# Block-diagonal attention with stationary probabilities, and batches 0 and 1 in 512-byte rows with f32 weights cast on chip

## The chip, the cores and the metric

The kernel runs on one core of one Trainium2 chip. The metric is the time of one execution in device microseconds. Before the change it took 377.15 us (median of three runs, 373.92 to 379.12).

Short names: PE is TensorE, DVE is VectorE, ACT is ScalarE, POOL is GpSimd, SP is SyncE, which here only issues DMAs. A *pass* is one matmul of 512 columns.

## The reference

Sliding-window attention over 8 batches of 8 heads, 576 positions and head size 64 (a position sees 32 positions to each side), then a dense layer pair with a squared relu.

```python
scores = q @ k.T / 8;  scores = where(|i - j| <= 32, scores, -1e9)
x = softmax(scores) @ v                   # (8, 8, 576, 64) -> 4608 tokens x 512
h = maximum(x @ w_in, 0)                  # 512 -> 2048
out = (s * h * h + b) @ w_out             # 2048 -> 512, s and b are one number each
```

q, k and v are drawn as 0.1 times a normal, so the scores are near zero and the softmax near uniform.

The constant `b` gives every token the same row `b * sum(w_out)`, called the constant row below (`CVEC`).

## The kernel before

The kernel does not write its instructions in order. It describes tasks (engine, cost, what they read and write), and a list scheduler in the kernel's own Python turns them into one fixed order per engine. The costs in the tasks decide the order; nothing is reordered when the kernel runs. Every engine works through its order and waits on semaphores.

```python
def plan(self):                           # before; [...] marks cuts
    [...]
    c = (max(free[s], t.ready), t.key, t.n)          # earliest start first
    [...]
    free[t.stream] = st + t.cost
    if t.dma is not None:                            # one DMA queue is modelled
        dma_free = max(dma_free, st + 1300.0) + t.dma[1]
        t.fin = dma_free + 700.0
    [...]

def load(b, n, blk, stream="sp", waits=()):          # q, k, v: 128 rows of 8 x 256 B
    [...]
    1070.0 if stream != "pool" else 1900.0, [...]
def load_weights(which, i, waits=()):                # POOL, f32 -> bf16 in the load
    e.dma_start(WIN_BF[:, :, i*512:(i+1)*512], moe_w_in[...])
def transpose_dma(b, n, blk):                        # q, k of batches 1 to 7, on SP
    e.dma_start(dst[:, :, s0:s0+ns], NAT[n][0:ns, blk, :], transpose=True)   # cost 1300

def unit(b, t, g2, after):                # 48 of them: 192 queries, 4 heads
    # PE: 8 matmuls q x k (64 rows deep)      -> SC
    # ACT: exp(SC) -> EX;  DVE: EX *= MASK
    # PE: 8 matmuls ONES x EX -> SS (the sums, 64 columns of weights)
    # PE: 8 matmuls V x EX    -> AV (already transposed: channels x tokens)
    # ACT: ln(SS), exp(-ln) -> REC;  DVE: XT = AV * REC
    [...]

def s1(m, ft): # PE: 4 passes w_in x XT -> W; ACT: relu -> R1; DVE: R1*R1 -> GT
def s2(m, sub, qd): # PE: 4 passes GT x w_out -> O; after 16: DVE -> OUTS, SP stores
```

The dense layers run over token blocks: 384, 128, then 512 tokens each. "The third block" is the first of 512 tokens.

The softmax here doesn't subtract the row's maximum and nothing guards it: scores larger than these inputs give would overflow.

Of the kernel before, what the change touches and what calls it, by code (L numbers as in the profile page):

```python
# [5 lines left out]
F32 = mybir.dt.float32  # L6
# [4 lines left out]
S = 576  # L11
# [6 lines left out]
NBLK = (S + 127) // 128  # L18
KCOLS = NBLK * 128
TOK = 512  # L20
# [4 lines left out]
class _Task:  # L25


    __slots__ = ("n", "stream", "fns", "cost", "lat", "key", "deps", "after", "users", "left",
                 "ready", "start", "fin", "dma", "sem", "seq", "val", "used", "snap")

    def __init__(self, n, stream, fns, cost, lat, key, dma):
        self.n, self.stream, self.fns, self.cost, self.lat, self.key, self.dma = \
            n, stream, fns, cost, lat, key, dma
        self.deps, self.after, self.users = set(), [], []
        self.ready = self.start = self.fin = 0.0
        self.sem = self.seq = self.val = None
        self.used = False
        self.snap = None


class _Graph:
# [3 lines left out]

    STREAMS = ("pe", "act", "dve", "pool", "sp")
    LAT = {"pe": 230.0, "act": 110.0, "dve": 90.0, "pool": 120.0, "sp": 60.0}

    def __init__(self, queues):
        self.queues = queues  # L50
        self.tasks = []
        self.writer, self.readers, self.named = {}, {}, {}

    def add(self, stream, fns, cost, reads=(), writes=(), key=0.0, accum=False, dma=None, waits=(),
            after=(), name=None, lat=None):


        if not isinstance(fns, list):
            fns = [fns]
        t = _Task(len(self.tasks), stream, fns, cost, self.LAT[stream] if lat is None else lat, key,  # L60
                  dma)
# [10 lines left out]
        t.after = list(after)  # L72
# [6 lines left out]
        if name is not None:  # L79
            self.named[name] = t  # L80
# [3 lines left out]
    def plan(self):  # L84
        free = {s: 0.0 for s in self.STREAMS}
        dma_free = 0.0
        for t in self.tasks:
            aft = [self.named[a] for a in t.after]
            t.left = len(t.deps) + len(aft)
            for d in t.deps:  # L90
                d.users.append((t, True))
            for d in aft:
                d.users.append((t, False))
        open_ = {s: [] for s in self.STREAMS}
        for t in self.tasks:
            if t.left == 0:
                open_[t.stream].append(t)
        order = []
        while len(order) < len(self.tasks):
# [10 lines left out]
            free[t.stream] = st + t.cost  # L110
            if t.dma is not None:
                dma_free = max(dma_free, st + 1300.0) + t.dma[1]
                t.fin = dma_free + 700.0
            else:
                t.fin = st + t.cost
            order.append(t)
            for u, hard in t.users:
                u.left -= 1
                if hard and u.stream == t.stream and t.dma is None and t.stream == "pe":
                    r = t.fin  # L120
                elif hard:
                    r = t.fin + (100.0 if t.dma is not None else t.lat)
                else:
                    r = t.start
                u.ready = max(u.ready, r)
                if u.left == 0:
                    open_[u.stream].append(u)
        self.order = order

    def emit(self, sems):  # L130


# [5 lines left out]
        plan = []  # L138

# [12 lines left out]
        for t in self.order:  # L152
            s = t.stream
            need = {}
            for d in t.deps:
                if s == "pe" and d.stream == "pe" and d.dma is None:
                    continue
                want(s, d, need)
            if t.dma is not None:
# [50 lines left out]
def bass_sliding_window_symmetric__then__act_starrelu_kernel(  # L210
# [12 lines left out]
    NT3 = S // 192  # L223

    sizes = [384, 128]
# [8 lines left out]
    with ExitStack() as es:  # L234
# [6 lines left out]
        def ps(shape, nm, dt=F32):  # L241
            uid["n"] += 1
            return es.enter_context(nc.psum_tensor(f"{nm}_{uid['n']}", list(shape), dt))

        WIN_BF = sb((128, 4, DFF), BF16, "win")
        WOUT_BF = sb((128, 16, DM), BF16, "wout")
        XT = sb((128, NPAIR, T), BF16, "xt")
        STG = {n: sb((128, NBLK, DM), F32, "stg" + n) for n in "qk"}
        STG["v"] = sb((128, 2 * NT3, DM), F32, "stgv")
        NAT = {n: sb((128, NBLK, DM), BF16, "nat" + n) for n in "qk"}  # L250
        VB = [sb((128, 2 * NT3, DM), BF16, "vb") for _ in range(2)]
        QT = [sb((128, NPAIR, S), BF16, "qt") for _ in range(2)]
        KT = [sb((128, NPAIR, S + 2 * WIN), BF16, "kt") for _ in range(2)]
        EX = [sb((128, 2, 512), BF16, "ex") for _ in range(2)]
        MASK = sb((128, 2, 512), BF16, "mask")
        LNS = [sb((128, 384), F32, "lns") for _ in range(2)]
        REC = [sb((128, 384), F32, "rec") for _ in range(2)]
        ONES = sb((128, 3, 64), BF16, "ones")
        ONESW = sb((128, 128), BF16, "onesw")
        IDENT = sb((128, 128), BF16, "ident")  # L260
        ZERO_F = sb((128, 1), F32, "zero")
        GT = [sb((128, 16, 512), BF16, "gt") for _ in range(2)]
        R1 = [sb((128, 512), BF16, "r1") for _ in range(4)]
        OUTS = [sb((128, DM), F32, "outs") for _ in range(3)]
# [6 lines left out]
        AV = ps((128, 512), "av")  # L271
        SS = ps((128, 512), "ss")
        BANKS = {("W", 0): W[0], ("W", 1): W[1], ("O", 0): O[0], ("O", 1): O[1]}

        queues = {"w": [f"dmaW{i}" for i in range(10)], "l": [f"dmaL{i}" for i in range(24)],
                  "a": [f"dmaA{i}" for i in range(8)], "o": [f"dmaO{i}" for i in range(8)],
# [6 lines left out]
        def rows(blk):  # L283
            return min(128, S - blk * 128)


        src_of = {"q": q, "k": k, "v": v}

        def load(b, n, blk, stream="sp", waits=()):
            if n == "v":  # L290
                k0 = 192 * (blk // 2) - WIN + 128 * (blk % 2)
                p0, p1 = max(0, -k0), min(128, S - k0)
                s0 = k0 + p0
            else:
                p0, p1 = 0, rows(blk)
                s0 = 128 * blk
            ns = p1 - p0
            return add(
                stream,
                lambda e: e.dma_start(  # L300
                    STG[n][p0:p1, blk, :].rearrange("p (h d) -> p h d", h=H),
                    src_of[n][b, :, s0:s0 + ns, :].rearrange("h s d -> s h d"),
                ),
                1070.0 if stream != "pool" else 1900.0, writes=[("STG", n, blk)],
                key=16 * (b - 2), waits=waits,
                dma=({"sp": "l", "act": "a", "pool": "w"}[stream], ns * 9.3))

        def load_weights(which, i, waits=()):
            if which == "in":
                fn = lambda e: e.dma_start(  # L310
                    WIN_BF[:, :, i * 512:(i + 1) * 512],
                    moe_w_in.rearrange("(kc p) f -> p kc f", p=128)[:, :, i * 512:(i + 1) * 512])
            else:
                fn = lambda e: e.dma_start(
                    WOUT_BF[:, 4 * i:4 * i + 4, :],
                    moe_w_out.rearrange("(fc p) c -> p fc c", p=128)[:, 4 * i:4 * i + 4, :])
            return add("pool", fn, 1000.0, writes=[("W" + which, i)], waits=waits, key=-50,
                       dma=("w", 2550.0))


        first = {}
        plan0 = [("q", 0, "sp"), ("k", 0, "act"), ("q", 1, "sp"), ("k", 1, "act"), ("v", 0, "sp"),
                 ("v", 1, "act"), ("q", 2, "sp"), ("k", 2, "act"), ("k", 3, "sp"), ("v", 2, "act"),
                 ("v", 3, "sp"), ("q", 3, "act"), ("q", 4, "sp"), ("k", 4, "act"), ("v", 4, "sp"),
                 ("v", 5, "sp")]
        for n, blk, stream in plan0:
            first[n, blk] = load(0, n, blk, stream)

        add("dve", lambda e: e.memset(ZERO_F[:], 0.0), 100, writes=["ZERO"], key=-99)
        add("dve", lambda e: e.memset(ONESW[:], 1.0), 150, writes=["ONESW"], key=-99)  # L330
        add("dve", lambda e: e.memset(ONES[:], 1.0), 150, writes=["ONES"], key=-99)
        add("dve", lambda e: e.memset(ONES[0:WIN, 1, :], 0.0), 100, writes=["ONES"], key=-98)
        add("dve", lambda e: e.memset(ONES[128 - WIN:128, 2, :], 0.0), 100, writes=["ONES"], key=-98)
        for slot in range(2):
            for c0 in (0, WIN + S):
                add("dve", lambda e, slot=slot, c0=c0: e.memset(KT[slot][:, :, c0:c0 + WIN], 0.0), 150,
                    writes=[("KTPAD", slot)], key=-98)
        for (p0, blk) in ((0, 0), (128 - WIN, 2 * NT3 - 1)):
            add("dve", lambda e, p0=p0, blk=blk: e.memset(STG["v"][p0:p0 + WIN, blk, :], 0.0), 350,
                writes=[("STGPAD", blk)], key=-98)  # L340
        add("pool", [lambda e: e.dma_start(SB128[:, 0:1], moe_s.partition_broadcast(128)),
                     lambda e: e.dma_start(SB128[:, 1:2], moe_b.partition_broadcast(128))],
            2000.0, writes=["SB128"], dma=("w", 200.0), key=-60)

        def band(tile, res, lo, hi):

            add("pool",
                lambda e: e.affine_select(tile, ONESW[:, :], pattern=[[1, 128]],
# [68 lines left out]
        def blocks(lo, hi):  # L417
            return range(lo // 128, (hi - 1) // 128 + 1)
# [224 lines left out]
```

## Time and profile before

| | before |
|---|---|
| median of three runs | 377.15 us |
| span of the profiled execution | 373.8 us |
| PE busy | 319.2 us (85%) |
| first 128x512 matmul of the third token block | 99.25 us |
| PE idle before 100 us / from 100 to 260 us | 40.1 / 10.0 us |

From the page of the kernel before: busy time by engine, then two rows of the 40 equal slices of the span (one digit a slice, tenths; `PEclk` is the clock granted to TensorE).

```profile
span 373.8 us, 6108 instructions
...
PE 319.2 (85%) x2385; PEld 155.5 (42%) x2424; DVE 193.2 (52%) x439; ACT 206.4 (55%) x310; POOL 44.7 (12%) x62
...
PE   1277985935499999988898899989999999999996
...
PEclk9999998975599999999999999999999999999999
```

PE is full from about the twelfth slice on. What the kernel loses lies in the first 100 us. The view by windows gives the same in microseconds: the window, its length, busy time (and count) of PE, weight loads, DVE, ACT and POOL, then the granted clock, the DMA share and GB/s.

```profile
0.00:30.00 30.00, 11.33 (x132) 7.75 (x134) 14.30 (x41) 11.30 (x16) 5.31 (x15) 1.00 1.00 164
30.00:60.00 30.00, 24.49 (x170) 12.76 (x168) 10.46 (x27) 16.03 (x29) 8.78 (x11) 1.00 1.16 199
60.00:100.00 40.00, 24.04 (x236) 14.67 (x240) 23.70 (x61) 17.08 (x29) 12.81 (x15) 0.69 1.20 212
100.00:260.00 160.00, 149.99 (x1205) 70.28 (x1224) 101.15 (x228) 110.25 (x161) 17.82 (x21) 0.99 1.03 180
```

PE idle is the window's length less PE busy: 18.7, 5.5, 16.0, then 10.0 us in the 160 us that follow. PE's waits in the kernel before (what waited and for what: total us, times, longest):

```profile
PE ss L458 <- DVE ex L445: 20.1, 13, 2.0
PE w L402 <- DVE natq L379: 6.0, 2, 5.3
...
PE o L543 <- DVE cvec L567: 4.0, 1, 4.0
PE sc L435 <- DMA kt<-natk: 3.7, 2, 2.0
```

11.8 of the 20.1 us are batch 1's six units, one after another between 75 and 97 us. The third block then starts (from the timeline of PE):

```profile
99.25 4.92 PE L525 MATMUL w<-xt,win 128*128 128x512 bf16 x14 [3.27 <-DVE xt L472]
```

### The profile page before, as it was taken

Reading aid. Unit: us, or ns where it says so; the run is one execution under the profiler, and the core shown is the slowest. Engines: PE = TensorE matmul, PEld = TensorE weight load, DVE = VectorE, ACT = ScalarE, POOL = GpSimd, SP = SyncE. Lnnn points to the kernel's source line nnn. Section 1 sums busy time; section 2 is a strip of 40 time slices with the busy share of each in tenths; the row PEclk is TensorE's granted clock in tenths of the full one; section 3 lists DMA queues with packets and bytes.
Section 4 is the critical chain, followed back from the end, with each engine's and each line's share of the span. In section 5 each row is a group of like instructions: output and inputs, shape, how many; then the busy total and the mean of one; then the engine's idle time right before and its main releaser. Section 6 shows DMA issues by size and latency. Waiting matters only on the chain.

```text
span 373.8 us, 6108 instructions
## 1 busy us (share of the span) xinstructions
PE 319.2 (85%) x2385; PEld 155.5 (42%) x2424; DVE 193.2 (52%) x439; ACT 206.4 (55%) x310; POOL 44.7 (12%) x62
## 2 busy tenths in 40 slices
PE   1277985935499999988898899989999999999996
PEld 0144543523244444443444344434444444444442
DVE  4363525745556775676585586454444453333321
ACT  1266732255368678767677576657676764434300
POOL 3012241342221210121111000000000000000000
PEclk9999998975599999999999999999999999999999
DMA  8979999999999999999899798863000001001012
GB/s 164 208 110 187 190 225 206 202 190 213 230 221 147 180 200 231 186 198 193 188 172 213 132 174 174 189 141 89 28 31 31 28 30 56 28 30 56 28 58 84
DMA packets 127869, 52.71 MB, mean 141 GB/s; under 512 B 116672, under 2 KB 120768, under 8 KB 127840
## 3 DMA queue, kind: packets, MB, share of 16 engines
q1 hardware_dynamic: 113648, 36.32, 54.2%
q0 software_dynamic: 7424, 14.29, 19.8%
q10 hardware_dynamic: 6768, 1.70, 2.7%
q8 instruction: 19, 0.31, 0.4%
q14 instruction: 10, 0.08, 0.1%
HBM read 38.80 MB, written 9.44 MB: 129 GB/s over the span
## 4 chain that ended last, share of the span: by engine, by line
PE 54%; DMA 19%; SPq 9%; DVE 7%; ACTq 3%; ACT 3%; issue 2%; DVEq 0%
PE o L543 25%; PE w L525 22%; DMA stgq<-in_q_dram 12%; DMA stgk<-in_k_dram 7%; SPq L300 6%; ACTq L300 3%; SPq L387 3%; PE ss L458 3%; PE sc L435 2%; DVE ex L445 2%; PE av L458 2%; ACT ex L442 1%; DVE xt L472 1%; DVE vb L379 1%; DVE gt L534 1%
## 5 line engine op out<-in xcount | busy, mean ns | idle before, releaser
L525 PE MATMUL w<-xt,win 128*128 128x512 bf16 (+2 forms) x624 | 146.4, 367 | 5.5 <-DVE xt L472 4.2
L543 PE MATMUL o<-wout,gt 128*128 128x512 bf16 x554 | 141.5, 382 | 6.0 <-DVE cvec L567 4.0
L525 PEld LDWEIGHTS w<-xt,win 128*128 128x128 bf16 x640 | 59.4, 100 | 71.8 <-issue 5.1
L543 PEld LDWEIGHTS o<-wout,gt 128*128 128x128 bf16 x576 | 53.2, 98 | 65.5 <-DVE cvec L567 4.2
L442 ACT ACTIVATE ex<-sc,zero 128x1024 bf16<-128x1024 f32 x48 | 53.2, 1109 | 12.1 <-PE sc L435 12.1
L445 DVE TENSOR_TENSOR ex<-ex,mask 128x1024 bf16<-128x1024 bf16 x48 | 33.0, 688 | 33.2 <-ACT ex L442 32.7
L300 POOL DMA_DIRECT2D stgv<-in_v_dram x42 | 35.7, 853 | 120.5 <-DVE vb L379 111.5
L465 ACT ACTIVATE lns<-ss,zero 128x384 f32<-128x384 f32 x48 | 27.7, 578 | 27.6 <-PE ss L458 27.5
L531 ACT ACTIVATE r_29<-w,zero 128x512 bf16<-128x512 f32 (+2 forms) x40 | 25.7, 643 | 30.7 <-PE w L525 30.6
L458 PE MATMUL ss<-ex,ones 128*64 128x128 bf16 x384 | 22.1, 244 | 20.5 <-DVE ex L445 20.1
L531 ACT ACTIVATE r_28<-w,zero 128x512 bf16<-128x512 f32 (+2 forms) x40 | 25.7, 642 | 23.1 <-PE w L525 22.6
L531 ACT ACTIVATE r_31<-w,zero 128x512 bf16<-128x512 f32 (+2 forms) x40 | 25.7, 644 | 23.0 <-PE w L525 22.0
L531 ACT ACTIVATE r_30<-w,zero 128x512 bf16<-128x512 f32 (+2 forms) x40 | 25.7, 643 | 19.2 <-PE w L525 18.8
L555 DVE SCALAR_TENSOR_TENSOR outs<-o,sb_36,cvec 128x512 f32<-128x512 f32 x36 | 26.8, 746 | 13.2 <-PE o L543 12.8
L472 DVE TENSOR_TENSOR xt<-av,rec 128x384 bf16<-128x384 f32 x48 | 26.5, 552 | 11.5 <-ACT rec L468 11.2
L379 DVE CAST natq<-stgq 128x512 bf16<-128x512 f32 (+1 forms) x40 | 17.2, 432 | 25.3 <-DMA stgq<-in_q_dram 25.0
L458 PEld LDWEIGHTS ss<-ex,ones 128*64 128x64 bf16 x384 | 13.6, 119 | 39.6 <-DVE ex L445 26.7
L468 ACT ACTIVATE rec<-lns,zero 128x384 f32<-128x384 f32 x48 | 29.3, 610 | 0.8
L435 PE MATMUL sc<-qt,kt 64*128 64x128 bf16 x384 | 21.2, 237 | 9.0 <-ACT qt L407 5.3
L534 DVE TENSOR_TENSOR gt<-r_29 128x512 bf16<-128x512 bf16 (+2 forms) x40 | 15.8, 396 | 22.7 <-ACT r_29 L531 22.7
L534 DVE TENSOR_TENSOR gt<-r_31 128x512 bf16<-128x512 bf16 (+2 forms) x40 | 15.8, 396 | 22.3 <-ACT r_31 L531 22.0
L534 DVE TENSOR_TENSOR gt<-r_30 128x512 bf16<-128x512 bf16 (+2 forms) x40 | 15.8, 394 | 18.6 <-ACT r_30 L531 18.6
(43 smaller groups left out, 134.4 us busy)
## 6 DMA issues: line engine op xcount, KB each, us to landing
out_dram<-outs SPq DMA_DIRECT2D x36, 256.0 KB, 2.3
stgq<-in_q_dram SPq DMA_DIRECT2D x31, 256.0 KB, 5.8
stgk<-in_k_dram SPq DMA_DIRECT2D x29, 256.0 KB, 6.0
stgv<-in_v_dram POOLq DMA_DIRECT2D x28, 256.0 KB, 5.7
stgv<-in_v_dram POOLq DMA_DIRECT2D x14, 192.0 KB, 5.9
win<-in_moe_w_in_dram POOLq DMA_DIRECT2D x4, 512.0 KB, 6.4
wout<-in_moe_w_out_dram POOLq DMA_DIRECT2D x4, 512.0 KB, 5.8
stgq<-in_q_dram SPq DMA_DIRECT2D x8, 128.0 KB, 5.9
```

The lines of the kernel that those rows point to most:

```text
L300: lambda e: e.dma_start(STG[n][p0:p1, blk, :].rearrange("p (h d) -> p h d", h=H), src_of[n][b, :, s0:s0 + ns, :].rearrange("h s d -> s h d ...
L435: fns.append(lambda e, u=u, pr=pr, a=a, hh=hh: e.matmul(SC[:, hh, 256 * u + 128 * a:256 * u + 128 * a + 128], lhsT=KT[slot][64 * hh:64 * h ...
L442: add("act", lambda e: e.activation(EX[e_][:, :, :], SC[:, :, :], AF.Exp, bias=ZERO_F[:, :], scale=0.125), 1130.0, reads=["SC", "ZERO"], w ...
L445: add("dve", lambda e: e.tensor_tensor(EX[e_][:, :, :], EX[e_][:, :, :], MASK[:, :, :], ALU.mult), 700.0, reads=[("E", e_), "MASK"], write ...
L458: fns.append(lambda e, u=u, a=a, hh=hh, dst=dst, lhs=lhs: e.matmul(dst[64 * hh:64 * hh + 64, 192 * u + 64 * a:192 * u + 64 * a + 128], lhs ...
L465: add("act", lambda e: e.activation(LNS[e_][:, :], SS[:, 0:384], AF.Ln, bias=ZERO_F[:, :], scale=1.0), 600.0, reads=["SS", "ZERO"], writes ...
L468: add("act", lambda e: e.activation(REC[e_][:, :], LNS[e_][:, :], AF.Exp, bias=ZERO_F[:, :], scale=-1.0), 600.0, reads=[("LNS", e_), "ZERO ...
L472: add("dve", lambda e: e.tensor_tensor(XT[:, prs[0]:prs[1] + 1, x0:x0 + 192], AV[:, 0:384].rearrange("p (u c) -> p u c", u=2), REC[e_][:, ...
L525: add("pe", [lambda e, kc=kc: e.matmul(W[wb][:, 0:nt], lhsT=WIN_BF[:, kc, ft * 128:(ft + 1) * 128], rhs=XT[:, kc, t0:t0 + nt], start=(kc = ...
L531: add("act", lambda e: e.activation(R1[rb][:, 0:nt], W[wb][:, 0:nt], AF.Relu, bias=ZERO_F[:, :], scale=1.0), 280 + 0.82 * nt, reads=[("W", ...
L534: add("dve", lambda e: e.tensor_tensor(GT[gs][:, ft, 0:nt], R1[rb][:, 0:nt], R1[rb][:, 0:nt], ALU.mult), 160 + 0.53 * nt, reads=[("R1", rb ...
L543: add("pe", [lambda e, fc=fc: e.matmul(O[ob][:, :], lhsT=GT[gs][:, fc, sub * 128:sub * 128 + 128], rhs=WOUT_BF[:, fc, :], start=(fc == 0), ...
```

## The change

Its intent is, in the start, to bring everything in sooner: q and k of batches 0 and 1 in rows of 512 bytes (two positions at a time), v without overlap, the weights as f32 in 2 KB rows, all on SP's queue in order of need, with casts on DVE and ACT. In the rest, it makes attention cheaper: K is stored block-diagonally so that a score matmul serves two heads with a depth of 128, and the probabilities are the stationary operand of the second matmul. A column of ones in V then gives the sums in the same matmul, so the `ss` matmuls and ACT's `ln` and `exp` go. The price is that the result comes out as tokens x channels and needs a transpose (on PE for batch 0, by DMA on SP for batches 1 to 7), and that K must be copied into its block-diagonal place (DVE). The scheduler changes too: it simulates two DMA rings, and has new costs.

```diff
-    def plan(self):                            # one pass, one DMA queue
+    def plan(self, rounds=5):                  # order and rings, five times
+        self._order(); self._rings()
+    LAT = {"pe": 260.0, "act": 130.0, ...};  MARGIN = 250.0
+    def _rings(self): [...]
+        self.land[j[0].n] = now + 1100.0 - j[0].start
 # loads of batches 2 to 7, cost of issuing and of the packets
-    1070.0 if stream != "pool" else 1900.0 [...] ns * 9.3
+    600.0, [...] dma=("l", ns // 2, 18.3)
 # q and k transposes on SP
-    1300.0, [...] dma=("t", 700.0)
+    1250.0, [...] dma=("t", ns // 4, 22.0)
+def pairs_chunk(b, name, t0, n, ...):   # batches 0, 1: 512 B rows
+    # SP load -> ACT (q) or DVE (k) cast -> 8 PE transposes
+    # -> q: 2 ACT copies to QT;  k: 4 DVE copies to KBD
+def load_weights(which, i, x, key, eng): # SP load f32 -> STG, cast by DVE or ACT
+def chunk(b, c, key):                    # batches 2 to 7
+    # 2 SP loads -> DVE cast -> 2 SP transposes -> 2 DVE copies KT -> KBD
+    add("dve", [KBD <- KT] 320, [...] key=key + 3.0, slack=2000.0)
 def unit(b, m):                            # 40 of them: 128 queries, 8 heads
+    # PE: 4 matmuls KBD x QT a 64-key tile -> SC; ACT exp; DVE mask (EXE, EXO)
+    # PE: 4 x (2 or 3) matmuls EX x VBD (130 columns) -> AVN; DVE 1/sum, DVE XN
+    # batch 0: 4 PE transposes, ACT copy;  else: SP transpose XN -> XT, cost 1250
 def colsum():
+    # POOL: 11 additions sum 12 of the 16 pieces of w_out; PE does the rest
[...]
```

Token blocks are now 128, 384, then 512.

## The prediction

> **What bounds it now.** TensorE, but only from 99 us on. The windows table has PE 319.2 us busy of 373.8. The MLP needs 1,152 passes of 512 columns; in the last 76 us (chain of waits) four take 0.86 us, so 249 us. Attention costs three groups of 8 matmuls per unit, about 0.35 us each start to start: 48 units, 50 us. Most of the other 74 us lie at the start. The PE timeline has the first MLP matmul at 31.9 us, waits for the constant row (4.0) and output weights (1.1), then from 75 to 97 us batch 1's six attention units one after another with 2 us holes at clock 0.50, and the third token block only at 99.25. Cause: batch 1's q and k, issued from 42 us beside casting weight loads, land over 50 us. In the packet records 256 B take 25 ns and a casting 1 KB write 105 ns (about 10 GB/s an engine), 2 KB take 90 ns (23 GB/s). From 99.25 on there are 274.5 us for about 259 of PE work: 11 lost, 4 of tail.
>
> The Trainium skill, "DMA: Bandwidth & Descriptors", Specifications, puts line rate at 512 B and more; the packet times agree about 256 B; no 512 B packet is in this trace.
>
> **What changes.**
> - Start: batches 0 and 1 in 512 B rows, v without overlap, weights in 2 KB f32 rows. Estimated 28 ns for 512 B and 90 for 2 KB: 13 us a batch, weights 22. All is in by 50 to 55 us instead of about 95.
> - The start's new limit: weight casts, strided copies into block-diagonal K. From the measured 686 ns (ACT, 512 f32) and 437 ns (DVE cast) I estimate 54 us of ACT and 60 of DVE before the third block. It starts at 70 to 75 us: 26 us gained.
> - PE per batch: 36 score and 52 AV matmuls of about 130 columns. The 128-column MLP block here runs 8 in 0.45 us, a weight load each: 56 ns, so 5 to 5.5 us against 6.3. Six batches: 5 us gained.
> - ACT loses ln and its exp (57 us) and gains copies. DVE rises from 193 to about 230 us, 27 of 37 per steady batch.
> - DMA per steady batch: v shrinks, output transposes come (about 2,300 256 B packets): 29 us against 37 of PE. SP issue, 16 transposes of 1.25 us and 10 loads, about 30 us: tight.
>
> **Prediction.** 73 us to the third block, 253 of PE work, 12 of stalls, 4 of tail: 342 us, range 327 to 362. Faster by over 2%: 0.95; within 2%: 0.04; slower: 0.01.
>
> **What would show it.** PE timeline: third block near 73 us, first MLP matmul still near 30. Packet records: 512 B near 28 ns. Lines: score and AV near 56 ns a matmul start to start. Windows: DVE 65 to 80% in the steady part, ACT and DVE nearly full from 10 to 65 us. PE waits after the third block under 15 us.
>
> **What would make it wrong.** SP's queue, in order and nearly full, delivers transposes late and PE waits for XT each batch: 360 or more. DVE delays the squares, and with three relu buffers ACT and PE follow. Or the start is bound less than I think and the third block runs by 60 us: 325 to 330.

## The result, and the profile after

| | before | after |
|---|---|---|
| median, runs of the same chip | 375.82 us | 393.19 us (392.8 to 394.81, four runs) |
| span of the profiled execution | 373.8 us | 393.1 us |
| PE busy | 319.2 us | 320.8 us |
| PE idle in all | 54.6 us | 72.2 us |
| PE busy at half clock | 14.3 us | 34.3 us |
| third token block starts | 99.25 us | 100.90 us |

The ratio is 1.0545, 95% interval 1.0474 to 1.0615: slower. Ratios here and below are the mean time of one kernel's runs over that of the other's of the same rounds, so not quite the ratio of the medians. Executions over 1.5% slower than the fastest of the same kernel are left out of the means.

The 19.3 us between the two spans can be added up. Idle is the span less PE busy; a microsecond of PE at half clock loses half a microsecond. Idle gives +17.6, the half clock (34.3 - 14.3) / 2 = +10.0, and what is left, PE's work at full clock, -8.3 us. So attention did become cheaper on PE, and more than that was lost in waits.

The same lines of the page after:

```profile
span 393.1 us, 5493 instructions
...
PE 320.8 (82%) x2007; PEld 173.0 (44%) x2042; DVE 219.8 (56%) x508; ACT 167.5 (43%) x280; POOL 61.7 (16%) x81
...
PE   2454577639998499984899589799999999999996
...
PEclk9997588859999889996999699899999999999999
```

The row of PE now has dents in its middle, and the clock row has dents with them. The view by windows of the kernel after:

```profile
0.00:30.00 30.00, 11.68 (x100) 8.97 (x100) 21.76 (x43) 18.65 (x23) 11.74 (x22) 1.00 1.05 285
30.00:60.00 30.00, 17.77 (x152) 11.98 (x150) 22.34 (x37) 18.10 (x30) 19.51 (x19) 0.72 1.05 269
60.00:100.00 40.00, 28.47 (x254) 19.41 (x257) 26.35 (x75) 18.90 (x43) 6.24 (x8) 0.79 1.10 172
100.00:260.00 160.00, 134.11 (x794) 68.72 (x808) 92.06 (x225) 65.11 (x106) 24.19 (x32) 0.93 0.94 172
```

Two things went wrong. Up to 100 us PE is idle 42.1 us (before 40.1), although far more bytes come in early: 285 GB/s against 164 in the first 30 us. From 100 to 260 us it is idle 25.9 us where before it was 10.0, and busy at half clock for 15.6 us (before 2.7). PE's waits after:

```profile
PE avn L551 <- DVE exo L536: 24.9, 7, 6.9
PE sc L526 <- DVE kbd L479: 8.9, 4, 3.2
PE o L463 <- ACT nat L456: 6.1, 1, 6.1
PE sc L526 <- DMA qt<-nat: 5.6, 1, 5.6
```

and, from the waits of DVE, the two for DMAs that turn out to be behind the first of them:

```profile
DVE nat L495 <- DMA stg<-in_k_dram: 32.1, 14, 4.5
DVE kbd L504 <- DMA kt<-nat: 21.3, 9, 5.3
```

One such stall, read first from the timeline of DVE (start, length, instruction, and in brackets the idle time before it and what ended it):

```profile
131.36 0.41 DVE L665 TENSOR_TENSOR gt<-r 128x512 bf16<-128x512 bf16 x1
135.83 0.46 DVE L504 COPY kbd<-kt 64x256 bf16<-64x256 bf16 x2 [4.07 <-DMA kt<-nat]
136.30 0.42 DVE L536 TENSOR_TENSOR exe<-exe,mask 128x512 bf16<-128x512 bf16 x1
136.65 0.42 DVE L536 TENSOR_TENSOR exo<-exo,mask 128x512 bf16<-128x512 bf16 x1
```

and then from that of PE:

```profile
130.63 1.03 PE L657 MATMUL w<-xt,win 128*128 128x512 bf16 x4
137.12 0.29 PE L551 MATMUL avn<-vbd,exo 128*128 128x130 bf16 x1 [5.47 <-DVE exo L536]
```

DVE stands for 4.07 us in front of a K copy whose transpose has not landed. Behind it wait the masks of another unit; behind the masks waits PE, in whose order that unit's AV matmuls come next. 5.47 us of PE are lost although dense passes were to be had: the next four in PE's order had their last operand, a `gt`, at 121.33 us. The waits view names DVE's masks, but the mask is only the last link; DVE's own waits show the DMA. This agrees with the Trainium skill, "PSUM — Partial Sum Buffer", Engine vs sequencer instructions: the queues of ScalarE, VectorE and GpSimdE are strictly first in, first out, and matmuls keep program order. The loss goes on after the wait: the clock record has TensorE at half clock for 6.83 us from 134.17 on. Stretches of the same length follow at 178.55 and 219.51.

The third block, from the timeline of PE:

```profile
100.90 0.38 PE L657 MATMUL w<-xt,win 128*128 128x512 bf16 x1
```

### The profile page after: what moved, and what is told of

Its sections match the earlier page's. It is cut to its first block, busy times and chain, and to the rows that moved or that the text cites. A ratio compares the mean times of both kernels' runs of the same rounds, so it can differ in the third digit from the quotient of the medians.

```text
span 393.1 us, 5493 instructions
## 1 busy us (share of the span) xinstructions
PE 320.8 (82%) x2007; PEld 173.0 (44%) x2042; DVE 219.8 (56%) x508; ACT 167.5 (43%) x280; POOL 61.7 (16%) x81
## 4 chain that ended last, share of the span: by engine, by line
PE 47%; DMA 23%; SPq 15%; DVE 10%; issue 3%; ACT 1%; DVEq 0%
PE o L674 23%; PE w L657 19%; DMA stg<-in_k_dram 13%; SPq L499 6%; DMA kt<-nat 4%; PE avn L551 4%; SPq L581 3%; PE sc L526 2%; SPq L489 2%; SPq L424 2%; DMA stg<-in_q_dram 2%; DMA qt<-nat 2%; DVE xn L563 2%; DMA stg<-in_moe_w_out_dram 1%; DMA stg<-in_moe_w_in_dram 1%
## 5 line engine op out<-in xcount | busy, mean ns | idle before, releaser
L663 ACT ACTIVATE r<-w 128x512 bf16<-128x512 f32 (+2 forms) x160 | 88.0, 555 | 157.9 <-PE w L657 133.7
L665 DVE TENSOR_TENSOR gt<-r 128x512 bf16<-128x512 bf16 (+2 forms) x160 | 63.8, 404 | 61.8 <-ACT r L663 61.0
L424 POOL DMA_DIRECT2D vst<-in_v_dram x48 | 36.6, 769 | 135.3 <-ACT vbd L437 113.5
L551 PE MATMUL avn<-vbd,exo 128*128 128x130 bf16 (+1 forms) x256 | 34.2, 240 | 21.0 <-DVE exo L536 17.4
L526 PE MATMUL sc<-qt,kbd 128*128 128x128 bf16 (+1 forms) x288 | 25.5, 234 | 19.4 <-DVE kbd L479 8.9
L495 DVE CAST nat<-stg 128x1024 bf16<-128x1024 f32 (+1 forms) x30 | 21.0, 704 | 32.1 <-DMA stg<-in_k_dram 32.1
L551 PEld LDWEIGHTS avn<-vbd,exo 128*128 128x128 bf16 (+1 forms) x256 | 26.2, 116 | 27.7 <-DVE exo L536 20.1
L551 PE MATMUL avn<-vbd,exe 128*128 128x130 bf16 (+1 forms) x160 | 30.8, 241 | 7.5 <-DVE exo L536 7.5
L686 DVE SCALAR_TENSOR_TENSOR outs<-o,sb,cvec 128x512 f32<-128x512 f32 x36 | 26.7, 742 | 12.2 <-PE o L674 12.2
L526 PEld LDWEIGHTS sc<-qt,kbd 128*128 128x128 bf16 x288 | 20.5, 106 | 29.2 <-DVE kbd L479 9.8
L534 ACT ACTIVATE exe<-sc 128x512 bf16<-128x512 f32 (+1 forms) x40 | 22.2, 554 | 23.5 <-PE sc L526 23.4
L504 DVE COPY kbd<-kt 64x512 bf16<-64x512 bf16 (+1 forms) x60 | 17.0, 283 | 23.6 <-DMA kt<-nat 21.3
L563 DVE TENSOR_TENSOR xn<-avn,rec 128x512 bf16<-128x512 f32 (+1 forms) x40 | 27.3, 683 | 1.7 <-DMA xt<-xn 1.2
```

Of the source, the lines that this page charges most:

```text
L424: land["v", b, h] = add(stream, lambda e: e.dma_start(VST[p0:p0 + 64, :, h // 2, :], v[b, h, :, :].rearrange("(t p) d -> p t d", p=64)), 6 ...
L495: add("dve", lambda e: e.tensor_copy(NAT[ni][0:ns, :, :].rearrange("p i c -> p (i c)"), STG[si][0:ns, :]), 680.0, reads=[("STG", si)], wai ...
L526: add("pe", [lambda e, j=j, pr=pr, lo=lo, hi=hi, c0=c0, w=w, par=par: e.matmul(SC[:, par, pr * 128 + c0:pr * 128 + c0 + w], lhsT=KBD[:, pr ...
L534: add("act", lambda e, src=src, dst=dst: e.activation(dst, src, AF.Exp, bias=0.0, scale=0.125), 190 + 0.833 * 4 * w, reads=[("SC", par)], ...
L551: fns.append(lambda e, pr=pr, buf=buf, col=col, j=j, x=x, last=len(parts) - 1: e.matmul(AVN[0:nr, pr, 0:130], lhsT=buf[:, pr, col:col + nr ...
L563: add("dve", lambda e: e.tensor_tensor(XN[xi][0:nr, :].rearrange("p (a b c) -> p a b c", a=4, b=2), AVN[0:nr, :, 0:128].rearrange("p a (b ...
```

## The experiments

All sixteen kernels give results within the comparison's tolerance. Each was timed beside the kernel before on the same chip; the ratio is to that. The medians of before in the four sets were 375.39, 373.15, 373.98 and 375.12 us. In the two sets of e5 to e8 and e13 to e16 the kernel before spread by 1.9% and 3.0%, and some of its runs counted as slow. Kernels of different sets are therefore best compared by their ratios and intervals.

The first theory was the one that the prediction had named as its main risk: **SP's queue is full** (theory A in the expectations). In the 200 us from 60 to 260 us the issues on SP, added up from the trace, take 188.3 us, and the change adds 37 transposes XN to XT there, 58 us of issuing. One number speaks against it from the outset: in the kernel before they take 186.4 us of the same stretch, and PE is idle there for only 10.0 us from 100 us on. Its rivals: the DMA engines' data rate (B); DVE's sharing with POOL (C), with POOL's additions in the start; **the plan's order**, which puts instructions that wait for DMAs ahead of others on DVE (D); and, for the start, the chains of casts and copies.

### e1: half of SP's loads moved to POOL

```diff
-    add("sp",   lambda e: e.dma_start(STG[si][...], q or k, batches 2 to 7), 600.0, dma=("l", ...))
+    add("pool", lambda e: e.dma_start(STG[si][...], q or k, batches 2 to 7), 900.0, dma=("v", ...))
```

> Edit: the 60 q and k loads of batches 2 to 7 are issued by POOL instead of SP; the same bytes and packets, the planned order remade. Theory A (SP's in-order issue is full from 60 to 260 us and everything behind it comes late): SP loses about 45 us of issue, lateness of the plan shrinks, 393 falls to 360 to 380. Theory B (the DMA engines' data rate, 256 B packets, is the limit): the bytes are the same, so 388 to 398. Theory C (VectorE's in-order queue and its sharing with POOL hold PE up, not the transfers): no better, or worse by the POOL traffic, 390 to 405.

Measured: 391.95 us, ratio 1.0414 (1.0338 to 1.0491). PE is idle 21.7 us from 100 to 260 us, hardly less than the 25.9. Taking 60 issues off SP bought about one per cent: the amount of work on SP isn't the cause.

### e2: the new transposes on PE instead of SP

```diff
-    add("sp", [XT <- XN, transpose=True], 1250.0)           # batches 1 to 7
+    add("pe", [4 transposes XN -> spare part of AVN], 300)
+    add("act", [XT <- AVN part], 190 + 0.833 * 4 * n)
```

> Edit: the attention output of batches 1 to 7 is transposed by TensorE and copied by ACT, as for batch 0, instead of by 37 DMA transposes on SP. SP loses 58 us of issue and the DMA engines about 19,000 packets of 256 B; PE gains about 9 us of work, ACT 20. Theories A and B: 360 to 380. Theory C: PE work added, nothing released: 395 to 405.

Measured: 392.54 us, ratio 1.0441 (1.0375 to 1.0507). All that the change had added to SP after the start is gone, and almost nothing is gained (idle from 100 to 260 us 19.5 us, but 140 more transposes for PE). With e1 this is against the theory of the full queue.

### e3 and e8: sixty tiny loads more on SP

```diff
+    add("sp", lambda e: e.dma_start(DUM[0:16, 4*d:4*d+4], q[0, 0, 0:16, 0:4]), 1.0, ...)
     # one beside each q or k load of batches 2 to 7
     # e8 only: waits=list(g.tasks[-1].deps), so it can't be planned ahead of that load
```

> Edit: 60 loads of 256 bytes are added to SP's queue between the q and k loads of batches 2 to 7; nothing reads them, and the plan is told that they cost nothing. About 0.35 us of issue each, 21 us on SP, next to no bytes. Theory A: 405 to 415. Theory B: under 3 us, 393 to 397. Theory C: the same as B.

> Edit: as e3, but each tiny load now depends on what its neighbour load waits for, so that the 60 stand in SP's queue from 45 us on (in e3 the plan had put them all at 20 to 45 us, where they delayed the start). About 0.42 us of issue each, 25 us on SP in all. Theory A (SP issue is the limit): 410 to 418. Theory B or D with SP having room: 393 to 399.

e3 measured 414.66 us, ratio 1.1078 (1.0993 to 1.1164), but it is misplaced: the scheduler, seeing nothing that a tiny load has to wait for, put them between 16 and 43 us into the start, and the third block came 27 us later (128.39 us). It says nothing about the rest. e8 has them in place: 404.19 us, ratio 1.0881 (1.0726 to 1.1035), so 11 us more than the change, between the two forecasts. In its trace the sixty take 42.4 us (a mean of 0.71 us, not the 0.42 expected), but other issues get shorter, and all of SP's issuing grows only from 244.9 to 253.3 us: an issue's time in the trace is not a fixed cost. SP's time is not free, then, when the plan doesn't know of it; but SP's busy time as such didn't pay when removed.

### e4: the column sum back on PE

```diff
-    for fc in range(1, 12): add("pool", [CSUM += WOUT_BF[:, fc, :]], 1200)
+    add("pe", [16 passes ONESW x WOUT_BF[:, fc, :]], 16 * 216)      # as before
```

> Edit: the column sum of the output weights is made by 16 TensorE matmuls as in the kernel before, not by 11 POOL additions and 5 matmuls. In the trace the VectorE casts of the output weights that run beside the POOL additions take 1.04 us, those of the input weights 0.67. Theory C: the start loses its VectorE slow stretch, 3 to 8 us gained, 385 to 390. Theories A and B: SP and the transfers are as before, within 2 us of 393.

Measured: 395.09 us, ratio 1.0514 (1.0442 to 1.0585): nothing gained. DVE's casts of `w_out` fell from a mean of 1038 to 694 ns, so they had been slowed beside POOL's additions, but those of `w_in` rose from 672 to 848 ns, and the third block came at 103.78 us.

### e5 and e6: DVE's DMA waits, moved later or moved away

e5 tells the scheduler to leave 10 us instead of 2 between the landing of a K transpose and its copies on DVE. e6 moves those copies and the casts of q and k, for batches 2 to 7, from DVE to POOL.

```diff
# e5
-    key=key + 3.0, slack=2000.0)
+    key=key + 3.0, slack=10000.0)
# e6
-    add("dve", [KBD <- KT], 320)        ;  add("dve", [NAT <- STG], 680)
+    add("pool", [KBD <- KT], 700)       ;  add("pool", [NAT <- STG], 1350)
```

> Edit: one number of the plan: the copies of K into block-diagonal form are placed in VectorE's order as if their transposes landed 10 us later instead of 2 us. The same instructions on the same engines. Theory D (these copies stand in VectorE's in-order queue before their transposes have landed, so the masks, and behind them PE, wait for transfers that have 20 us of slack): VectorE's wait for the K transposes (21 us) falls under 6, PE's wait for the masked probabilities (25 us) under 12, 375 to 385. Rate theory (A or B: SP issue or the DMA engines' rate): the waits move elsewhere, 388 to 398.

> Edit: for batches 2 to 7 the block-diagonal K copies and the q and k casts, which wait for transfers, run on POOL instead of VectorE. Theory D: VectorE waits for no transfer any more in the steady part, PE's waits there fall from 26 us to about 10, 372 to 382, unless POOL's slower copies make transposes late. Rate theory: 388 to 398. Sharing of VectorE and POOL (theory C): masks and squares slow down beside POOL's copies, 393 or more.

e5: 390.56 us, ratio 1.0482 (1.034 to 1.0624). The wait that it aimed at went from 21.3 us to none, and the sister wait grew. PE's wait for masks (`exo`) from 100 to 260 us fell only from 22.9 to 19.4 us. DVE's waits in e5 are

```profile
DVE nat L495 <- DMA stg<-in_k_dram: 37.3, 19, 6.7
...
DVE nat L459 <- DMA stg<-in_k_dram: 8.0, 5, 3.5
...
DVE nat L495 <- DMA kt<-nat: 2.9, 1, 2.9
```

The theory as stated for e5 fell. e6: 375.25 us, ratio 1.0112 (1.0016 to 1.0208), about 17 us faster than the change; PE's idle time from 100 to 260 us falls to 12.8 us, its half clock in the whole run from 34.3 to 21.6 us. POOL does the same work more slowly (614 ns a K copy instead of 283), and it helps. Now POOL stands in front of the late loads and transposes, and the masks pass:

```profile
POOL nat L495 <- DMA stg<-in_k_dram: 35.1, 10, 5.3
...
POOL kbd L504 <- DMA kt<-nat: 20.0, 10, 5.0
```

This points to DVE waiting in order for DMAs, and moving one of the two waits isn't enough. By itself e6 would also fit a DVE with too much work; e7, which leaves all of that work on DVE, excludes this.

### e7, e9, e10: the same instructions, planned with measured costs

No instruction of the kernel after is changed; only numbers that the scheduler reads. The trace after has a k load's issue at a mean of 0.67 us and a q load's at 0.81 (median 0.58), a transpose's at 1.50 to 1.58 us (median 1.26). The plan had 0.60 and 1.25: about the medians, and for the transposes a fifth below the mean. Landing times were too short as well.

```diff
# issue costs (e7, e9)
-    600.0, [...q, k loads]     1250.0, [...q, k transposes]     1250.0, [...XN transposes]
+    780.0, [...]               1530.0, [...]                    1580.0, [...]
# transfer costs (e7, e10)
-    dma=("l", ns // 2, 18.3)   dma=("t", ns // 4, 22.0)   self.land[...] = now + 1100.0 - ...
+    dma=("l", ns // 2, 25.0)   dma=("t", ns // 4, 28.0)   self.land[...] = now + 1600.0 - ...
```

> Edit: only the costs in the plan: SP issue 1.53 and 1.58 us for transposes and 0.78 for loads (measured means) instead of 1.25 and 0.60, 256 B packets dearer, half a us more to land. Theory D and any theory of a wrong order: waits of PE shrink, 375 to 387. Rate theory: 390 to 396.

> Edit: of e7's costs in the plan only those of SP issue (1.53, 1.58 and 0.78 us). If what was wrong in the plan is SP's issue time: 355 to 365, as e7. If it is how late transfers land: 380 to 393.

> Edit: of e7's costs in the plan only those of the transfers (dearer 256 B packets, 0.5 us more to land), SP issue as in the changed kernel. If what was wrong is how late transfers land: 355 to 365, as e7. If it is SP's issue time: 380 to 393.

e7: 358.0 us (356.89 to 361.92), ratio 0.9656 (0.9547 to 0.9766). It is 35 us below the median of the change, which was timed in another set (by the two ratios, 8%), beats the kernel before, and is faster than any of its forecasts. By windows:

```profile
0.00:30.00 30.00, 11.05 (x89) 8.46 (x90) 21.32 (x43) 18.23 (x22) 11.89 (x22) 1.00 1.06 277
30.00:60.00 30.00, 19.44 (x159) 13.56 (x158) 21.95 (x36) 19.17 (x32) 19.42 (x19) 1.00 1.06 274
60.00:100.00 40.00, 30.34 (x270) 18.94 (x275) 27.93 (x82) 21.08 (x46) 7.65 (x10) 0.96 1.05 173
100.00:260.00 160.00, 158.01 (x1006) 83.44 (x1025) 109.88 (x268) 78.33 (x130) 23.49 (x31) 1.00 0.95 182
```

and its waits of DVE for DMAs:

```profile
DVE kbd L504 <- DMA kt<-nat: 15.6, 9, 3.2
...
DVE nat L459 <- DMA stg<-in_k_dram: 8.0, 5, 3.3
...
DVE nat L495 <- DMA stg<-in_k_dram: 4.9, 4, 1.9
```

From 100 to 260 us PE is idle 2.0 us instead of 25.9, at full clock. SP is just as full (191.1 us of issues from 60 to 260 us against 188.3) and the DMA share is the same (0.95 against 0.94), so neither was the limit. DVE still waits for K transposes, but its wait for k loads fell from 32.1 to 4.9 us, and its waits no longer reach PE. PE's wait for masks in this stretch, in the change and in e7:

```profile
PE avn L551 <- DVE exo L536: 22.9, 6, 6.9
```

```profile
PE avn L551 <- DVE exo L536: 0.2, 1, 0.2
```

e9, issue costs alone: 367.31 and 364.9 us, ratio 0.9805 (0.9717 to 0.9892). e10, transfer costs alone: 385.76 us, ratio 1.0297 (1.0214 to 1.038). Most of the gain is in the issue costs; both together give more. In e10's trace, from 100 to 260 us, DVE's wait for k loads fell from 27.5 to 8.2 us, its wait for K transposes stayed (20.4 and 20.5), and PE is idle 18.5 us. Comparing the plan's own start times with the trace, on DVE, says the same: the kernel after was about 16 us behind its plan at 100 us, 36 at 190 and 51 at 260; e7 was about 12 us behind at 100 us and stayed so. One execution of e9, the profiled one, took 674.64 us. Its clock is listed as 1.0 and its page has no clock row, yet its `o` passes took a mean of 678 ns (391 in the change). So e9 has no usable profile, and, a further run being slow (370.95), it is judged by the two runs alone.

### e11: the kernel before, planned with measured costs

```diff
-    t.fin = dma_free + 700.0     1070.0 [...] ns * 9.3     2550.0 [weights]     1300.0, dma=("t", 700.0)
+    t.fin = dma_free + 1200.0    1270.0 [...] ns * 11.0    3300.0               1490.0, dma=("t", 800.0)
```

> Edit: the kernel before, with the costs in its own plan raised to what its trace shows (SP issue 1.27 us a load and 1.49 a transpose, a load 1.41 us of transfer, weights 3.3, 0.5 us more to land). If any kernel gains from an honest plan, and the change itself brings nothing: 355 to 362, as e7. If the order was only wrong in the changed kernel, whose VectorE has more that waits for transfers: 368 to 378.

Measured: 370.79 us, ratio 0.9935 (0.9871 to 0.9998). The kernel before gains under one per cent from the same treatment, although its plan had been wrong too: the trace is about 16 us behind it at 100 us, 22 at 190 and 30 at 260. DVE waited for DMAs in the kernel before as well, 19.4 us from 100 to 260 us (the change: 47.9); in e11 these waits are gone, and PE's idle time there falls from 10.0 to 5.3 us. So a wrong plan and DMA waits on DVE need not cost much. Why they cost the kernel after so much more, whether by their length or by what stands behind them, isn't shown. With measured costs on both sides, the change is worth 358.0 against 370.8 us (ratios 0.9656 and 0.9935), over two sets of runs.

### e12: the start of e7, with the weight casts on POOL and the column sum on PE

```diff
-    load_weights(which, i, x, nxt(), ("dve", "act")[x])
+    load_weights(which, i, x, nxt(), "pool")                 # and e4's edit
```

> Edit: e7, and in the start the 16 weight casts run on POOL instead of VectorE and ACT, with the column sum on TensorE. If the casts that wait for weights in VectorE's and ACT's queues hold up batch 0's and 1's attention: PE's idle time from 30 to 100 us (20 us in e7) falls by 5 to 8, 350 to 354. If sharing with POOL or the arrival of data rules there: 356 to 362.

Measured: 358.81 and 362.69 us, ratio 0.9661 (0.9563 to 0.976): no gain over e7. One further run was slow (368.44), and the profiled execution took 430.12 us at a clock of 0.76, so where its time lies isn't known.

### e13, e14: what holds the start

At this point the third block was still unexplained: 95.86 us in e7, 100.90 in the change, against a predicted 73, with all loads in by about 56 us. e13 is e7 with one part of the change undone: the weights again by casting loads on POOL, held back until batch 0's v and last k have landed. e14 is e7 without batch 1's q and k work.

```diff
# e13
-    add("sp", [STG <- weights f32], 600.0);  add("dve" or "act", [bf16 <- STG])
+    add("pool", [bf16 <- weights, cast in the load], 1000.0, dma=("w", 16, 105.0),
+        waits=[land["v", 0, 7] if which == "in" and i == 0 else land["k", 0, 512]])
# e14
-    qk(1, 0, 128)    qk(1, 256, 128)    qk(1, 512, 32)
-    rhs=QT[slot][...]
+    rhs=QT[0 if b == 1 else slot][...]
```

A slip in the first of these expectations: the weight casts are 16 in all, 8 on each engine, and in e7 take 7.5 us of DVE and 8.4 of ACT.

> The kernel after with the measured plan costs of e7, and one part of the change undone: the weights are again loaded by casting loads on the POOL queue (held back until batch 0's v, then batch 0's last k, has landed), so VectorE and ScalarE lose the 16 weight casts each had in the start (about 15 us each) and the staging buffers are free for q and k. If the on-chip weight casts hold up the start: third token block near 88 us instead of 95.9, and 350 us in all (e7: 358.0). If batch 0's and batch 1's own chain of copies holds it: 94 us or later, 355 to 360. If the casting loads delay everything as in the kernel before: later than e7, over 360.

> Wrong on purpose: e7, but batch 1's q and k are neither loaded, cast, transposed nor copied; batch 1's units read batch 0's (the result of batch 1 is wrong). PE loses 48 transposes (about 3 us of work), VectorE 3 casts and 12 copies into block-diagonal K, ScalarE 3 casts and 6 copies. If this chain holds the third block back: 86 to 89 us instead of 95.9, and 347 to 350 us in all, several us more than the 3 us of PE work. If it is not what holds it: 93 us or later, 355.

e13: 352.6 us, ratio 0.948 (0.9424 to 0.9537), which just doesn't touch e7's interval. e14: 350.17 us, ratio 0.9399 (0.9317 to 0.9481). e14 was also called correct: with scores this near zero, batch 0's in place of batch 1's stay within tolerance. It remains a wrong kernel, good only as an experiment. The third block in e7, e13 and e14, from the timelines of PE (in e14 with the window set after its last 384-column matmul, which would be merged with it):

```profile
95.86 1.89 PE L657 MATMUL w<-xt,win 128*128 128x512 bf16 x8
```

```profile
85.55 1.90 PE L653 MATMUL w<-xt,win 128*128 128x512 bf16 x7 [2.30 <-DMA xt<-xn]
```

```profile
80.79 1.03 PE L655 MATMUL w<-xt,win 128*128 128x512 bf16 x4
```

e13 moves the third block forward by 10 us and e14 by 15; over the whole profiled execution e13 takes 7.7 us less than e7 and e14 10.4 us less, of which an estimate of 3 us is the PE work of its transposes (48 of them, at the cost of one piece's eight, about 0.56 us in the plan). So the start hangs on these two: the weights' way through casts, and batch 1's chain of cast, transpose and copy; both share DVE and ACT. Neither engine is full there: in e7 from 30 to 60 us DVE is busy 73% and ACT 64%. What remains, as the likeliest reading, is a chain in which each step waits for the one before on another engine. The profile lines that speak for it are PE's waits for DVE's copies into block-diagonal K (`sc <- kbd L479`, 8.9 us in the change) and ACT's copies of q.

The planners, run again without the chip, add to this. The third block is planned at 84.2 us in e7, 83.1 in e13 and 76.0 in e14, and comes 11.7, 2.5 and 4.8 us later. So e13's gain comes nearly all from keeping closer to its plan, and about half of e14's from a shorter plan. One lateness of e7 is in the traces: DVE's wait for the k loads of batches 0 and 1 (`nat L459`) is 8.0 us there, 1.3 in e13 and 2.7 in e14. Whether that is the whole of it was not tested.

e13 changes three things at once, the casts, the staging buffers and 16 loads on SP, and e14 drops batch 1's q and k loads with the chain; the runs don't separate them. Nor is it known why e12, which took the casts off DVE and ACT too, gained nothing.

### e15, e16: the parts together

e15 is e7 with e6's edit; e16 is e13 with e6's edit.

> e7 and e6 together: measured plan costs, and the K copies and q/k casts of batches 2 to 7 on POOL instead of VectorE. The theory that e7 and e6 took away the same waits (VectorE held by late transposes) expects no further gain: 355 to 359 us, PE idle between 100 and 260 us about 2, as in e7. If they took away different ones: 345 to 350.

> e13 and e15 together, the candidate for the best version. Expected: what e13 gains over e7, plus nothing from the POOL copies once the start is over; from 80 us on POOL also does batch 2's copies, which leaves VectorE 8 us more room before 100 us. 345 to 357 us.

e15: 356.5 us, ratio 0.9555 (0.9486 to 0.9625), against 358.0 and 0.9656 for e7 in another set: the intervals overlap. e6 and e7 take away the same waits. Its profiled run was slow (361.08), so it isn't used. e16: 351.76 us, ratio 0.946 (0.9403 to 0.9517), the same as e13 within the intervals. The best correct versions are e13 and e16, 5% faster than the kernel before and about 10% faster than the change as it was written.

## Why the prediction was wrong

**"73 us to the third block" failed by 28 us.** Measured 100.90. The loads did what was predicted: 512-byte packets took a mean of 32.3 ns (median 29, predicted near 28; 256-byte ones 23.5, so twice the bytes for 1.4 times the time; the 2 KB ones took 92, so 512-byte rows did not reach their rate: 15.9 against 22 GB/s an engine), the weights' last load was issued at 38.7 us and landed at 44.8, and batch 1's q and k were in by about 56. The step that failed is the one after it. "54 us of ACT and 60 of DVE before the third block" was turned into a start at 70 to 75 us as if both engines could be kept nearly full from 10 to 65 us. The sums were about right (ACT 55.7 us busy up to 100 us, DVE 70.5, a sixth more than forecast), but the engines were 62% and 75% busy from 10 to 60 us. The reading is that they form a chain with PE, and a chain isn't bounded by the sum of its busiest engine. e13 and e14 show that relieving either part of that preparation moves the third block by 10 and 15 us; which link holds it stays open. The scheduler's own plan, looked at afterwards, has the third block at 84.4 us in the change and at 83.4 before: it wasn't even planned to start sooner. So some 11 of the 28 us were in the plan, and the other 16.5 are lateness against it.

**"12 of stalls" failed by about 22 us.** From 100.90 us to the end are 292.2 us. 30.2 of them are idle, of which 4.0 lie in the last 93 us and are mostly the tail; half clock costs 7.8. That is some 34 us lost instead of 12. The mechanism is shown by e7, with e6, e9 and e10 beside it: the static plan was made with issue and landing times that were too short, so the trace ran ever further behind the plan, DVE stood in its order in front of late transposes and loads, and masks, AV matmuls and dense passes stood behind it. With truer numbers in the plan and no other change the 25.9 us from 100 to 260 us became 2.0.

**"253 of PE work, 4 of tail" was right.** 292.2 - 30.2 - 7.8 leaves 254.2 us. Score and AV matmuls were predicted at 56 ns start to start. One AV group at full clock starts its first and its eighth matmul at

```profile
301.16 0.22 PE L551 MATMUL avn<-vbd,exe 128*96 128x130 bf16 x1
...
301.56 0.22 PE L551 MATMUL avn<-vbd,exo 128*96 128x130 bf16 x1
```

so seven steps in 0.40 us, 57 ns each, with 130 columns. That agrees with the Trainium skill, "TensorE: Matmul & The Clock Gate", section "Wait — 56ns, not 53.3ns?", which has 55.6 ns for 128 columns.

**"DVE about 230 us" and the loss of `ln`** were right: 219.8 us, and ACT fell from 206.4 to 167.5. DVE's share in the steady part, forecast as 65 to 80%, was 58% because the stretch was longer (69% in e7).

**The named risk was near, but not it.** The prediction said that SP's queue, nearly full, might deliver transposes late and PE would wait for XT each batch, 360 or more. Transposes were late. But it wasn't XT that PE waited for, and relieving SP (e1, e2) hardly helped, while e7 has SP as full and next to no stalls. The two misses, 28 and 22 us, make up the 51 us between 342 and 393.

## What to carry to other kernels

Where instructions are ordered ahead of time by a scheduler, its cost figures are part of the kernel: put measured means in them (raising the issue costs alone from about the medians to the means was worth 7%, e9 against the change), compare planned with actual start times, and see whether the lag grows; a growing lag is a reason to look, not yet a loss, as the kernel before shows. The plan's own end is no guide while its costs are too low: it was 342.6 us in the change and 344.5 in e7, which ran 35 us faster. When a wait names a cheap vector instruction, look at what that engine itself was waiting for; an in-order engine that serves both DMA arrivals and the matmuls' next operands passes the delay on. And moving bytes sooner gained nothing here (PE idle 42.1 us up to 100 us against 40.1), where a chain of casts and copies over three engines follows: count the chain's steps, not just each engine's sum.

## What the Trainium skill lacked or had wrong

- "TensorE: Matmul & The Clock Gate", Part 1, says that the clock halves after at least one idle window of about 3.4 us. In this trace, by its clock record and the modelled ends of matmuls, less was enough: in the stall at 131.66 us the half clock begins at 134.17, 2.5 us after PE's last matmul, and PE was busy for 0.9 of the 3.4 us before; ahead of the half clock at 62.49 us it was busy for 1.9 of them. The stretch from 134.17 lasts 6.83 us, 3.9 of them after PE is busy again, so the stall of 5.5 us cost about 2 us more in half-clock work (an estimate: half of 3.9).
- "DMA: Bandwidth & Descriptors", Issuing engines are not separate DMA queues, calls the time to initiate a DMA usually small relative to the DMA. For a DMA transpose of up to 128 rows it isn't small here: median 1.26 us, mean 1.50 to 1.58 us on SP, against medians of 2.6 to 3.9 us from issue to landing, and the issues filled SP from 60 to 260 us. That page has cycles for a transpose only for "previous generations", in a part about trn3. Nor did I find that issue times vary with the kernel around them: in e8 the means of the same transposes are 1.27 to 1.39 us.
- "SBUF — State Buffer", SBUF: two separate sides, describes the port pair that DVE and GpSimd lock against each other. The runs show a possible size for it in this kernel: DVE's 128x1024 casts of `w_out` took a mean of 1038 ns beside POOL's 512-column additions and 694 ns without them (e4). The lock itself isn't in the trace, the casts of `w_in` grew from 672 to 848 ns in the same run, and the time of the whole kernel didn't move.
- No page that I read has a figure for how far a single execution of a program on one core can be off: 674.64 us in e9 (its other runs 364.9 to 370.95) at a listed clock of 1.0, and 430.12 us in e12 (its other runs 358.81 to 368.44) at a granted clock of 0.76. Both were profiled executions on the same chip; the cause isn't known.
